# Attention and two feed-forward layers on one core: six raw weight tiles instead of five, one low-word buffer instead of two, three tiles of scaled first keys instead of four

## The chip, the core and the metric

The kernel runs on one core of one Trainium2 chip. The metric is the device time of one execution, in microseconds. TensorE (PE) does the matmuls and transposes, VectorE (DVE), ScalarE (ACT) and GpSimd (POOL) the elementwise work, and SyncE (SP) issues nearly all DMAs; PEld is the loading of weights into TensorE. Each engine works through its own list of instructions in order. An instruction that waits for a semaphore holds up everything behind it in its list.

## The reference

The inputs are q, k and v of 4 batches, 8 heads, 576 positions and 64 columns, a gate s per position, and five weight matrices in float32. What is computed, cut to what matters:

```python
cum  = cumsum(maximum(s, 0))
bias = minimum(-(cum[:, None] - cum[None, :]), 0)        # per head
a    = softmax(causal(q @ k.T / 8 + bias)) @ v           # 576 x 64 per head
x    = a, heads side by side                             # 2304 x 512
x    = (silu(x @ w_gate) * (x @ w_val)) @ w_out          # d_ff 1536
out  = silu(x @ w_in) @ w_out2                           # d_ff 2048
```

## The kernel before, in words

**Precision.** Every product is taken in three matmuls of the type fp32r: each operand is cut into a high part (rounded) and a low part (the rest), and high x high, high x low and low x high are summed in PSUM (`mm3`, L522 to L524). The rounding is a copy on ACT (L112), the rest a subtraction on POOL (L501 for weights, L535 for hidden units).

**Raw weight words.** The weights come from the host as 64-bit words, of which the device keeps 32 bits. A piece of 512 columns is loaded as a tile `r64` of 128 x 512 x 2 words (512 KB) and decoded: ACT writes the scaled high word into half of a 1024-column tile `zz` (L409) and the shifted low word into a buffer `dk` (L410); DVE joins the two (L412, L415). `r64`, `zz` and, later, the working tiles of the second layer's weights (`z32`, `s32`, `cut`) all live in one ring, the pool `raw`, 4 KB per partition each. One chunk of weights takes four `r64` and two `zz`. The buffer `dk` is in the pool `dec` for chunk 0 and for the second layer's weights (24 of 32 pieces); for the other chunks of the first layer it is a PSUM bank of the pool `ps_m`. That pool has four banks, and the outputs of the first layer's matmuls (`pgv`, `po`) and of the attention's value product (`pv`) take turns in the same four.

**Stages.** From 0 to about 60 us the attention of batch 0 runs alone. Then the first feed-forward layer runs batch by batch, nine chunks of weights each, with the attention of the next batch between its matmuls: a chunk takes about 18 us. During the nine chunks of batch 0 the next chunk is decoded and cut (`w_split`), the one after it loaded (`w_load`), and the cut weights are stored to DRAM (`w1_d`, L489) for batches 1 to 3. From about 233 us to 634 us the second layer's weights are decoded, combined, cut and stored (`ahead_load`, `ahead`, `u_sum`, `u_cut`, `u_store`). From about 640 us the second layer runs out of other tiles, laid where the first layer's were.

**Attention.** Per pair of heads there are two halves, A and B. For each tile of 128 queries: scores on PE (`psc`, L218), minimum with the gate on DVE (L235, result `m`), exponential on ACT (L255), the sum's inverse `rl` (L268), scaling of `e` on POOL (`normal`, L116), and, from batch 1 on, the first 64 keys scaled into an own tile `z` of 128 x 128 (`first_keys`, ACT for half A, POOL for half B). PE then transposes `e` and `z` into `ptr` (L302, L316), and multiplies by v (`pv`, L351). The small tiles `m`, `l`, `rl` are in the pool `sm`.

**What sets the order.** Up to about 60 us the order on every engine is that of the code. From there to the end of batch 2 PE's order is that of the code, and a scheduler places the instructions of ACT, DVE, POOL and SP by its own model of time and by when tiles of the pools come free (`manual_schedule(engines={PE})`). From the last batch of the first layer on, the order is again that of the code.

```python
# gate(), 2 banks per step, then silu_mul(): tanh on ACT (L531), (tanh + 1) * gate on DVE (L532), * value (L533)
for t in range(2):
    ps = ps_m.tile([P, 512], F32, tag="m", name="pgv")
# w_split(c): decode the four pieces, cut and store the two halves
# w_ahead(c), at the start of chunk c: w_split(c + 1), then w_load(c + 2)
```

Of the kernel before, what the change touches and what calls it, by code (L numbers as in the profile page):

```python
# [66 lines left out]
def kernel(  # L67
# [11 lines left out]
    first_layer = ctx.enter_context(ExitStack())  # L79
    attention = ctx.enter_context(ExitStack())  # L80
    second_layer = ctx.enter_context(ExitStack())

    def pool(name, bufs, space=None, scope=ctx, side="left"):
        kw = {"space": space} if space is not None else {}
        return scope.enter_context(tc.tile_pool(name=name, bufs=bufs, side=side, reuse_waits="tile", **kw))
# [2 lines left out]
    const = pool("const", 1)  # L88
    dram = pool("dram", 1, bass.MemoryType.DRAM)
    wt_p = pool("wt", 4)  # L90
    raw_p = pool("raw", 5, scope=first_layer)
    dec_p = pool("dec", 2, scope=first_layer)
    tmp_p = pool("tmp", 3, scope=first_layer)
    h_p = pool("h", 6, scope=first_layer)
    xt_p = pool("xt", 8, scope=first_layer)
# [1 line left out]
    qkr_p = pool("qkr", 3, scope=attention, side="right")  # L97
    cum_p = pool("cum", 3, scope=attention, side="right")
    e_p = pool("e", 6, scope=attention, side="right")
    z_p = pool("z", 4, scope=attention, side="right")  # L100
    pt_p = pool("pt", 3, scope=attention, side="right")
    zero_p = pool("zero", 1, scope=attention, side="right")
    v_p = pool("v", 2, scope=attention, side="right")
    sm_p = pool("sm", 10, scope=attention, side="right")
    ps_m = pool("ps_m", 4, PS)
    ps_a = pool("ps_a", 2, PS, scope=attention, side="right")

# [959 lines left out]
```

## Time and profile before

| what | us |
|---|---|
| three runs | 1009.87, 1007.95, 1001.23 |
| their median | 1007.95 |
| the profiled execution | 1002.95 |
| its span, first to last instruction | 1001.1 |
| PE busy / PEld busy | 989.5 / 929.8 |
| POOL, DVE, ACT busy | 592.7, 557.0, 523.0 |
| mean granted clock of TensorE | 0.998 |

The profiled execution is 5.0 us under the median of the three runs, which lie 8.6 us apart. A row of the trace gives an instruction's start in us from the span's start, its duration, its engine and source line, what it writes and reads, and in brackets how long its engine had been idle before it and which instruction ended that. Names are those of the program's tiles, without their numbers (`r` is an `r64`, `wraw` a `zz`, `w_d` is `w1_d`).

### The profile page before, as it was taken

How to read it: one execution, taken by the hardware profiler on the slowest of the kernel's cores; microseconds unless marked ns; L12 is line 12 of the kernel's file. 1: busy time of each engine (PE TensorE's matmuls, PEld its weight loads, DVE VectorE, ACT ScalarE, POOL GpSimd, SP SyncE). 2: the span in 40 equal slices, each digit the busy share in tenths (PEclk: the TensorE clock that was granted, in tenths of full speed). 3: DMA queues.
4: the chain of work that ended last, by engine and by line, in shares of the span. 5: the costliest groups of instructions: out<-in, count | busy, mean ns of one | idle time of the engine just before them, and what ended most of it. 6: DMA issues, size and time to landing. Idle time of an engine off the chain costs nothing.

```text
span 1001.1 us, 19462 instructions
## 1 busy us (share of the span) xinstructions
PE 989.5 (99%) x6924; PEld 929.8 (93%) x6924; DVE 557.0 (56%) x1408; ACT 523.0 (52%) x1267; POOL 592.7 (59%) x748
## 2 busy tenths in 40 slices
PE   8999999999999999999999999999999999999998
PEld 6588889999998899899899999999999999999998
DVE  6868576635546545535542323366666667665555
ACT  6779888535666436655533443234544335543333
POOL 6967747515867556757542665356567458674445
PEclk9999999999999999999999999999999999999999
DMA  8798879667779799775858776797767866896662
GB/s 240 198 319 301 275 277 301 222 221 246 279 267 294 266 306 311 265 248 214 288 205 330 270 297 258 261 388 278 294 242 281 312 222 249 297 343 232 244 219 113
DMA packets 81616, 267.16 MB, mean 267 GB/s; under 512 B 9904, under 2 KB 29360, under 8 KB 66160
## 3 DMA queue, kind: packets, MB, share of 16 engines
q1 hardware_dynamic: 81328, 265.66, 75.8%
q8 instruction: 54, 0.88, 0.3%
q14 instruction: 42, 0.34, 0.1%
q10 hardware_dynamic: 192, 0.27, 0.1%
HBM read 208.15 MB, written 57.75 MB: 266 GB/s over the span
## 4 chain that ended last, share of the span: by engine, by line
PE 90%; ACT 3%; DMA 3%; DVE 2%; issue 1%; POOL 1%; SPq 0%; DVEq 0%; ACTq 0%; POOLq 0%
PE pgv L522 9%; PE pgv L524 9%; PE pgv L523 9%; PE pu L663 6%; PE pu L666 6%; PE pu L667 6%; PE po L708 6%; PE po L709 6%; PE po L710 6%; PE po L522 5%; PE po L523 5%; PE po L524 5%; PE pv L351 5%; PE psc L218 4%; PE ptr L302 3%; ACT e L255 1%
## 5 line engine op out<-in xcount | busy, mean ns | idle before, releaser
L522 PE MATMUL pgv<-xt,wt 128*128 128x288 f32 x768 | 229.5, 299 | 0.2 <-DVE wraw L415 0.2
L524 PE MATMUL pgv<-xt,wt 128*128 128x288 f32 x768 | 226.1, 294 | 0.0
L523 PE MATMUL pgv<-xt,wt 128*128 128x288 f32 x768 | 226.0, 294 | 0.0
L640 POOL TENSOR_TENSOR h<-u,h 128x384 fp32r<-128x384 f32 x72 | 74.8, 1039 | 142.1 <-ACT h L112 134.5
L522 PEld LDWEIGHTS pgv<-xt,wt 128*128 128x128 f32 x768 | 144.1, 188 | 11.5 <-DVE m L235 6.3
L523 PEld LDWEIGHTS pgv<-xt,wt 128*128 128x128 f32 x768 | 144.1, 188 | 0.0
L524 PEld LDWEIGHTS pgv<-xt,wt 128*128 128x128 f32 x768 | 144.0, 188 | 0.0
L112 ACT ACTIVATE h<-u 128x288 fp32r<-128x288 f32 (+1 forms) x168 | 79.8, 475 | 100.5 <-DVE u L533 99.2
L535 POOL TENSOR_TENSOR h<-u,h 128x288 fp32r<-128x288 f32 x96 | 79.0, 825 | 86.4 <-ACT h L112 84.2
L522 PE MATMUL po<-h,wt 128*128 128x288 f32 x384 | 114.7, 299 | 0.0
L523 PE MATMUL po<-h,wt 128*128 128x288 f32 x384 | 113.1, 294 | 0.0
L524 PE MATMUL po<-h,wt 128*128 128x288 f32 x384 | 113.0, 294 | 0.0
L708 PE MATMUL po<-h,wt 128*128 128x384 f32 x336 | 112.4, 335 | 0.0
L709 PE MATMUL po<-h,wt 128*128 128x384 f32 x336 | 112.3, 334 | 0.0
L710 PE MATMUL po<-h,wt 128*128 128x384 f32 x336 | 112.3, 334 | 0.0
L663 PE MATMUL pu<-x,wt 128*128 128x384 f32 x330 | 111.8, 339 | 0.1
L666 PE MATMUL pu<-x,wt 128*128 128x384 f32 x330 | 111.8, 339 | 0.0
L667 PE MATMUL pu<-x,wt 128*128 128x384 f32 x330 | 111.7, 339 | 0.0
L640 POOL TENSOR_TENSOR h<-t,h 128x384 fp32r<-128x384 f32 x96 | 107.0, 1136 | 5.5 <-ACT h L112 5.5
L669 ACT ACTIVATE s<-pu 128x384 f32<-128x384 f32 x48 | 23.6, 492 | 150.0 <-PE pu L667 150.0
L255 ACT ACTIVATE e<-e,m 64x64 f32<-64x64 f32 (+4 forms) x160 | 88.3, 554 | 25.7 <-DVE m L235 25.0
L719 DVE TENSOR_TENSOR acc<-po,acc 128x384 f32<-128x384 f32 x144 | 76.8, 558 | 36.3 <-PE po L710 35.6
(115 smaller groups left out, 2187.0 us busy)
## 6 DMA issues: line engine op xcount, KB each, us to landing
wt<-w_d SPq DMA_DIRECT2D x54, 1024.0 KB, 6.9
wt<-wu_d SPq DMA_DIRECT2D x48, 1024.0 KB, 9.2
wt<-wu_d SPq DMA_DIRECT2D x47, 768.0 KB, 6.8
r<-in_w_dram SPq DMA_DIRECT2D x36, 512.0 KB, 6.8
w_d<-wt SPq DMA_DIRECT2D x18, 1024.0 KB, 8.5
r<-in_w_dram SPq DMA_DIRECT2D x64, 256.0 KB, 7.1
qkr<-in_qk_dram SPq DMA_DIRECT2D x32, 288.0 KB, 9.0
cumb<-cum_d SPq DMA_DIRECT2D x15, 576.0 KB, 9.2
```

Of the source, the lines that this page charges most:

```text
L112: act_last[:] = [nc.scalar.activation(out=out, in_=in_, func=AF.Copy, scale=scale).ins]
L255: nc.scalar.activation(out=e[:r, hd, :wd], in_=e[:r, hd, :wd], func=AF.Exp, bias=m[hd][:r], scale=-1.0, accum_out=put[hd],)
L522: nc.tensor.matmul(out=ps[:, :n], lhsT=a, rhs=xh, start=(k == 0), stop=False)
L523: nc.tensor.matmul(out=ps[:, :n], lhsT=a, rhs=xl, start=False, stop=False)
L524: nc.tensor.matmul(out=ps[:, :n], lhsT=c, rhs=xh, start=False, stop=(k == last))
L640: nc.gpsimd.tensor_tensor(out=h[:, 1], in0=u, in1=h[:, 0].bitcast(F32), op=ALU.subtract)
L663: nc.tensor.matmul(out=o, lhsT=a, rhs=x[:, 0, kk], start=fresh and kk == 0, stop=False, skip_group_check=True)
L666: nc.tensor.matmul(out=o, lhsT=a, rhs=x[:, 1, kk], stop=False, **more)
L667: nc.tensor.matmul(out=o, lhsT=c, rhs=x[:, 0, kk], stop=kk == 1, **more)
L708: nc.tensor.matmul(out=ps, lhsT=a, rhs=h[:, 0], start=fresh, stop=False, skip_group_check=True)
L709: nc.tensor.matmul(out=ps, lhsT=a, rhs=h[:, 1], stop=False, **more)
L710: nc.tensor.matmul(out=ps, lhsT=c, rhs=h[:, 0], stop=e == 1, **more)
```

## The change

Four numbers of tiles in pools: `raw` 5 to 6, `dec` 2 to 1, `z` 4 to 3, `sm` 10 to 8.

```diff
-    raw_p = pool("raw", 5, scope=first_layer)
-    dec_p = pool("dec", 2, scope=first_layer)
+    raw_p = pool("raw", 6, scope=first_layer)
+    dec_p = pool("dec", 1, scope=first_layer)
...
-    z_p = pool("z", 4, scope=attention, side="right")
+    z_p = pool("z", 3, scope=attention, side="right")
...
-    sm_p = pool("sm", 10, scope=attention, side="right")
+    sm_p = pool("sm", 8, scope=attention, side="right")
```

PE's list of 5749 rows is the same in both kernels. On ACT, DVE, POOL and SP the lists are the same up to about 60 us, and from there to the end of batch 2 the scheduler places instructions differently, mostly in the nine chunks of batch 0. In the rows below a tile's number tells it apart: `r64_1101`, `1103`, `1105`, `1107` are the four pieces of chunk 2, `r64_1295` to `1301` those of chunk 3; `u_1259` is the result of the last gate step of chunk 0, `u_1474` that of the third of chunk 1.

The list of ACT at the start of chunk 1 (about 70 to 78 us), before:

```order
L531 ACTIVATE u_1168<-pgv_1142 128x288
L409 ACTIVATE wraw_1265<-r64_1101 128x512
L409 ACTIVATE wraw_1265<-r64_1103 128x512
L112 ACTIVATE h_1030<-u_1168 128x288
L410 ACTIVATE dk_1266<-r64_1101 128x512
L410 ACTIVATE dk_1271<-r64_1103 128x512
...
L255 ACTIVATE e_1011,l_1222<-e_1011,m_1218 128x320
L531 ACTIVATE u_1259<-pgv_1233 128x288
L255 ACTIVATE e_1011,l_1222<-e_1011,m_1220 128x320
```

and with the change:

```order
L409 ACTIVATE wraw_1265<-r64_1101 128x512
L409 ACTIVATE wraw_1265<-r64_1103 128x512
L112 ACTIVATE h_1109<-u_1136 128x288
L531 ACTIVATE u_1168<-pgv_1142 128x288
L409 ACTIVATE wraw_1276<-r64_1105 128x512
L409 ACTIVATE wraw_1276<-r64_1107 128x512
L112 ACTIVATE h_1030<-u_1168 128x288
...
L255 ACTIVATE e_1011,l_1222<-e_1011,m_1218 128x320
L255 ACTIVATE e_1011,l_1222<-e_1011,m_1220 128x320
L531 ACTIVATE u_1259<-pgv_1233 128x288
```

All four high words are now taken ahead of `h_1030`, where two were, and the tanh of `u_1259` stands behind both exponentials of 128x320 instead of between them.

The list of ACT in the second half of chunk 1 (about 86 to 95 us), before:

```order
L112 ACTIVATE pt_1443<-ptr_1432 128x2x384
L267 ACTIVATE l_1356<-l_1356 128x2
L112 ACTIVATE h_1367<-u_1426 128x288
L409 ACTIVATE wraw_1512<-r64_1295 128x512
L409 ACTIVATE wraw_1512<-r64_1297 128x512
L531 ACTIVATE u_1474<-pgv_1448 128x288
L410 ACTIVATE dk_1513<-r64_1295 128x512
...
L409 ACTIVATE wraw_1523<-r64_1299 128x512
```

and with the change:

```order
L409 ACTIVATE wraw_1523<-r64_1299 128x512
L409 ACTIVATE wraw_1523<-r64_1301 128x512
L267 ACTIVATE l_1356<-l_1356 128x2
L112 ACTIVATE pt_1443<-ptr_1432 128x2x384
L112 ACTIVATE h_1367<-u_1426 128x288
L531 ACTIVATE u_1474<-pgv_1448 128x288
L410 ACTIVATE dk_1513<-r64_1295 128x512
```

The last two pieces of chunk 3 are read ahead of the tanh of `u_1474`, where they stood behind it.

The list of POOL in chunk 1 (about 78 to 91 us), as the difference:

```order
 L116 TENSOR_SCALAR e_1004<-e_1004,rl_1210 128x128 x2
+L116 TENSOR_SCALAR e_1011<-e_1011,rl_1225 128x256 x2
 L501 TENSOR_TENSOR wt_1287<-wraw_1265,wt_1287 128x1024
 L200 AFFINE_SELECT e_1566<-cumb_784 128x192 x2
 L535 TENSOR_TENSOR h_1109<-u_1259,h_1109 128x288
-L116 TENSOR_SCALAR e_1011<-e_1011,rl_1225 128x256 x2
 L501 TENSOR_TENSOR wt_1291<-wraw_1276,wt_1291 128x1024
```

The scaling of the last `e` tile of the half goes ahead of a weight cut, two masks and an `h`. In the same way SP issues the loads of chunk 3's last two pieces (`r64_1299`, `r64_1301`) ahead of the store of a cut weight tile that stood between them, and POOL writes the second `z` of a half B behind the masks of the next half instead of ahead of them.

## Rows read from the trace of the kernel before

**Rows 1.** Busy us (instructions) by stretch: PE, PEld, DVE, ACT, POOL, PEclk, DMA share, GB/s.

```profile
16.00:58.00 42.00, 39.06 (x337) 25.27 (x338) 34.22 (x131) 33.07 (x88) 39.06 (x72) 0.96 0.85 251
58.00:110.00 52.00, 51.06 (x394) 46.20 (x394) 37.27 (x106) 45.06 (x115) 34.42 (x51) 1.00 0.88 301
110.00:390.00 280.00, 280.00 (x2175) 254.33 (x2174) 154.22 (x471) 164.88 (x430) 160.25 (x242) 1.00 0.80 269
...
640.00:990.00 350.00, 349.90 (x2006) 349.61 (x2005) 218.03 (x370) 150.24 (x326) 204.97 (x182) 1.00 0.74 272
```

**Rows 2.** What PE waited for: us in total, times, longest us.

```profile
PE ptr L302 <- POOL e L116: 3.5, 6, 1.4
...
PE pgv L522 <- DVE wraw L415: 0.2, 1, 0.2
```

**Rows 3.** PE in order of time, four starts of groups of matmuls.

```profile
77.99 0.40 PE L522 MATMUL pgv<-xt,wt 128*128 128x288 f32 x1
...
85.46 1.00 PE L302 MATMUL ptr<-ident,e 128*128 128x128 f32 x4 [0.63 <-POOL e L116]
...
94.62 0.40 PE L522 MATMUL pgv<-xt,wt 128*128 128x288 f32 x1 [0.19 <-DVE wraw L415]
...
412.22 0.76 PE L351 MATMUL pv<-pt,vz 128*64 128x320 f32 x4 [0.61 <-DVE u L532]
```

**Rows 4.** DVE in order of time: what frees the banks of Rows 3.

```profile
77.51 0.43 DVE L532 SCALAR_TENSOR_TENSOR u<-u,pgv 128x288 f32<-128x288 f32 x1
...
93.88 0.68 DVE L415 SCALAR_TENSOR_TENSOR wraw<-r,dk 128x512 uint32<-128x512 uint32 x1
```

**Rows 5.** ACT in order of time, chunk 1.

```profile
72.66 0.67 ACT L409 ACTIVATE wraw<-r 128x512 f32<-128x512 f32 x1 [0.98 <-DMA r<-in_w_dram]
73.23 0.43 ACT L112 ACTIVATE h<-u 128x288 fp32r<-128x288 f32 x1
...
76.86 0.38 ACT L531 ACTIVATE u<-pgv 128x288 f32<-128x288 f32 x1
77.15 0.55 ACT L255 ACTIVATE e<-e,m 128x320 f32<-128x320 f32 x1
...
88.72 1.24 ACT L409 ACTIVATE wraw<-r 128x512 f32<-128x512 f32 x2
89.85 0.41 ACT L531 ACTIVATE u<-pgv 128x288 f32<-128x288 f32 x1
```

**Rows 6.** Issue of raw loads; us to landing, issued at 63.3, 66.5, 84.0.

```profile
66.09 1.39 SPq L388 DMA_DIRECT2D r<-in_w_dram  x2
...
r<-in_w_dram SPq DMA_DIRECT2D x1, 512.0 KB, 4.7
...
r<-in_w_dram SPq DMA_DIRECT2D x2, 512.0 KB, 6.7
...
r<-in_w_dram SPq DMA_DIRECT2D x1, 512.0 KB, 10.8
```

**Rows 7.** Stretches as in Rows 1: ACT in chunk 1; TensorE's clock.

```profile
78.00:90.00 12.00, 11.25 (x85) 10.82 (x84) 8.78 (x34) 12.00 (x32) 9.57 (x14) 1.00 0.85 256
...
14.00:16.00 2.00, 0.41 (x2) 0.14 (x1) 1.95 (x11) 1.72 (x6) 2.00 (x5) 1.00 0.85 227
...
18.00:20.00 2.00, 2.00 (x10) 0.98 (x10) 1.97 (x12) 2.00 (x7) 2.00 (x5) 0.50 1.04 289
```

**Rows 8.** What ACT waited for after 240 us, as in Rows 2.

```profile
ACT cut L112 <- DMA wu_d<-cut: 19.0, 7, 4.7
```

**Rows 9.** Buffer dk: DVE's last use of one, ACT's next write.

```profile
17.43 1.01 DVE L415 SCALAR_TENSOR_TENSOR wraw<-r,dk 128x512 uint32<-128x512 uint32 x1
...
18.76 0.65 ACT L410 ACTIVATE dk<-r 128x512 uint32<-128x512 uint32 x1
```

**Rows 10.** A half B's second z; the transposes that free its tile.

```profile
120.91 0.60 POOL L116 TENSOR_SCALAR z<-e,rl 128x64 f32<-128x64 f32 x2 [0.50 <-DVE rl L268]
...
122.19 0.49 PE L316 MATMUL ptr<-ident,z 128*128 128x128 f32 x3
```

## The prediction

> **What bounds the kernel now.** I read the table of stretches first. From 110 to 390 us and from 640 to 990 PE is busy all the time, at a granted clock of 1.00; gaps of more than a microsecond lie ahead of 110 [rows 1] or at the very end, where nothing is changed. The reader is to see that there is almost nothing to win on the other engines: ACT, DVE and POOL are busy half of the time, and each of their delays costs something only where it reaches PE. So I read next what PE waited for [rows 2]. The largest entry, 3.5 us in six waits for a scaled `e`, lies almost wholly before 60 us, where the order of every engine is that of the code. Behind 60 us just three waits are left, and the order in time shows them: 0.63 us at 85.46, 0.19 at 94.62 and 0.61 at 412.22 [rows 3]. Together that is 1.43 us, 0.14% of the time, and it is all that a better order behind 60 us can give back. PE's own list is unchanged, so no matmul is added or removed. A change in time must be a wait of PE that goes or comes.
>
> **The change part by part.** I measure against the profiled execution, 1002.95 us.
>
> *Sixth raw tile, in the first layer.* It frees the loads from the ring's tail and lets the scheduler take all four high words of a chunk earlier on ACT. What this meets is thin: the four PSUM banks that decoding shares with the matmuls. At 77.99 us PE starts chunk 1's first gate in the bank that the tanh of `u_1259` and DVE's multiply behind it have just left: DVE's L532 runs from 77.51 for 0.43, so the bank is free at 77.94 [rows 4], 0.05 us ahead of PE [rows 3]. There is no slack here, and the view of waits doesn't say so because nothing was late. Now I move ACT's list. Before, ACT waited 0.98 us for the second piece, read it at 72.66 and came to `h` at 73.23: a read is worth 0.57 [rows 5]. With the change ACT must have the third and fourth piece too before that `h`. They are issued no earlier than about 66.1 (the engine order puts two small loads ahead of them as before), and such a load landed after 4.7, 6.7 or 10.8 us [rows 6]. At 6.7, the middle one and that of the two loads issued at this very place, ACT has the third at 72.8 and is through both at 72.8 + 2 x 0.57 = 73.9, 0.7 late. The tanh then also stands behind one more exponential of 0.55 [rows 5]. 0.7 + 0.55 = 1.25 us: tanh at 78.1 instead of 76.86, bank free at 79.2, PE's gate at 79.2. **+1.25.** Bounds: at 4.7 us ACT is early by more than the exponential costs, so 0; at 10.8 us it is 4.1 us later, so 5.3.
>
> *The scaling of `e` moved ahead on POOL.* The 0.63 us at 85.46 is PE waiting for just the instruction that now stands ahead of the weight cut. **-0.63**, at worst 0. The weight cut that was ahead of it comes later by this one pair of instructions; PE first reads those weights when it starts chunk 2, at 94.62 [rows 3], and that lies nine microseconds behind. If this cover were gone, the chunk's start would be late by the length of the pair, which I bound by the 1.00 us that PE spent on the four transposes it releases.
>
> *Two more reads ahead of the tanh of `u_1474`.* ACT is full from 78 to 90 us, 12.00 of 12 [rows 7]. So it cannot make up the 1.25, and the pair of reads now ahead of the tanh adds what the pair at 88.72 took, 89.85 - 88.72 = 1.13 [rows 5]. Tanh at 89.85 + 2.4. The chain from it ends in DVE's L415 at 93.88, which frees the bank of PE's start at 94.62 [rows 3, 4]; PE was already 0.19 late there. All 2.4 pass through: PE starts chunk 2 at 97.0 instead of 94.62. Of these 2.4 us, 1.25 - 0.63 = 0.62 are already counted, so **+1.78** here. Bounds: 0, if DVE takes up the lateness, since the low words of the last two pieces are no longer interleaved with reads; and about 6, if the last piece again takes the 10.8 us it took behind a store [rows 6]. That store is now issued after it, hence the lower middle.
>
> *Later chunks of batch 0.* The same moves, but PE waited for a decode nowhere else: the entry is one wait of 0.2 us [rows 2]. Nothing in the sum; the price if this cover is gone is the third rival.
>
> *Sixth raw tile, in the second layer's weights.* ACT waited 19.0 us in seven waits for stores to leave tiles of the ring [rows 8]. Only one delay of this kind reached PE, at 412.22. With six tiles for the six that one round needs, it should go. **-0.61**, at worst 0.
>
> *One `dk`.* At the start DVE's last use of the other buffer ends at 18.44, and ACT writes the next at 18.76 [rows 9]: 0.3 us of cover; lost cover would cost one such DVE instruction, 1.0 us. In the second layer's weights pieces are a quarter of a chunk apart. 0.
>
> *Three `z`.* The second `z` of half B was written at 120.91, and the transposes that free its new tile are at 122.19 [rows 10]. It would wait 1.8 us on POOL with `e` behind it; the scheduler has put it behind the masks, so the wait falls where POOL has nothing PE needs soon. The reader is PE a chunk, 18 us, later. 0; the price if it blocked is that 1.8 us once. *Eight small tiles:* a minimum now waits for the exponential eight minima back instead of ten; 0.
>
> **Sum:** 1.25 - 0.63 + 1.78 - 0.61 = +1.8, so 1004.7 against the profiled 1002.95. That execution lies 5.0 us under the median of the runs, 1007.95, and the runs spread over 8.6 us without a cause in this profile. I take the middle of both for what three runs will show: 1004.7 + 2.5 = **1007**. This spread also says that about 1% is what can be told from no change.
>
> TensorE's clock fell to 0.50 from 18 to 20 us, the lower of its two levels, 1.2 instead of 2.4 GHz, after PE had been busy for only 0.41 of the 2 us from 14 to 16 [rows 7]; that cost half of 2 us. From 58 to 110 us, with the 0.63 us wait in it, it stayed at 1.00 [rows 1]. So I add nothing for the clock. The Trainium skill, "TensorE: Matmul & The Clock Gate", section "HAM oscillation — how this bites in real kernels", says that a PE that waits between groups of matmuls is slowed and starts the next group cold. By that rule my two new waits would each cost about the 1.0 us of that drop more, 1006.7 on the profiled base.
>
> **Rivals.** *Nothing reaches PE* (0.27): the loads land early, DVE absorbs the rest, or the sixth tile is not what the loads wait for at all, so that the change does not do what it says. Then only the three waits move: between -1.43 and 0, 1001.5 to 1003 on the profiled base, 1004 to 1005.5 in runs. For it: margins in the scheduler's plan are not mine; against it: the 0.05 us.
>
> *PE is not really full* (0.03). Loading of weights is busy 46.2 of 52 us and 254.3 of 280 us [rows 1], 31 us short in both; if a third of it were waits that the ring causes, the time would fall by 10 us, to 992. Against it: PE does 2175 matmuls in 280 us and 2006 in 350, where loading is full; the first are the narrower ones and go at 129 ns each, and 394 in the 51.1 busy us of 58 to 110 at 130, the same pace on both sides of the gaps. The Trainium skill, "Perfetto Trace Analysis", section "Identifying the Most-Contended Engine", says that matmul busy time is no good measure of the distance from the limit and names weight loading instead. By that rule these 31 us are headroom; the pace says it isn't waiting.
>
> *Slower* (0.08): the same late tanh at each start of chunks 3 to 8 as at chunk 2. The place is the shared banks; the price is 1.78 each, six times, 10.7 us: 1015.4 on the profiled base, 1018 in runs. It decides from the point at which ACT is as full as in chunk 1. Against it: 58 to 110 us holds 45 us of ACT in 52, later 165 in 280 [rows 1].
>
> **How the numbers follow.** My forecast has 0.62. The range starts at the lowest run less the three waits, 1001.23 - 1.43 = 999.8, and ends at the highest run plus half of the upper bounds' 6 us, about 1013; the slower rival and the headroom stay outside. Faster by over 1% needs the second rival or a lucky set of runs: 0.04. Slower by over 1% is the third rival and a little for the upper bounds: 0.09. The rest, 0.87, is within 1%.
>
> **What would show it.** In the changed profile PE should wait about 1.2 us for DVE at the first gate of chunk 1, near 78 us, and about 2 us at the start of chunk 2, near 95 to 97; the waits at 85 and 412 should be gone; ACT's waits for stores after 240 us should fall well under 19 us; PE should be busy all the time from 110 us on. It is wrong if PE waits in every chunk, if the end at 990 to 1001 us is longer, or if the waits before 60 us change, where no instruction moved.

## The result and the profile after

The changed kernel takes 1013.33 us, the median of 8 runs (1012.01 to 1014.77), against 1004.33 us of the kernel before in the same comparison (8 runs, 1001.23 to 1009.87): a ratio of 1.0087, 95% interval 1.0072 to 1.0101. It is slower by 9.0 us, where 1.8 us was forecast. The forecast time itself, 1007.0, stood on a higher base, since the three runs known then had a median of 1007.95; even so the result lies 0.3 us above the end of its range.

The profiled execution has a span of 1011.6 us. First the table of stretches, with the columns of [rows 1]:

```profile
16.00:58.00 42.00, 37.33 (x315) 23.96 (x314) 36.59 (x130) 31.57 (x86) 35.92 (x64) 0.92 0.79 242
58.00:110.00 52.00, 48.61 (x378) 43.34 (x379) 34.27 (x102) 43.47 (x109) 34.59 (x54) 1.00 0.88 295
110.00:390.00 280.00, 275.94 (x2133) 250.49 (x2133) 149.58 (x461) 162.87 (x423) 157.11 (x241) 0.99 0.78 260
640.00:990.00 350.00, 349.94 (x2025) 349.65 (x2024) 214.54 (x365) 147.15 (x318) 203.12 (x179) 1.00 0.75 277
```

From 640 us on nothing is different. From 58 to 390 us PE was idle for 0.9 us before and is idle for 7.5 us now; the clock has fallen somewhere behind 110 us; and from 16 to 58 us, where no instruction moved, PE was busy for 1.7 us less, at a mean clock of 0.92 instead of 0.96. The four largest of PE's waits behind 58 us (columns of [rows 2]; four shorter ones come to 1.8 us):

```profile
PE po L522 <- DVE xt L366: 2.0, 1, 2.0
PE pgv L522 <- DVE wraw L415: 1.5, 1, 1.5
PE pgv L522 <- DVE u L532: 1.5, 1, 1.5
PE po L522 <- DVE wraw L415: 1.2, 1, 1.2
```

Two of these four are the ones forecast, at the starts of chunks 1 and 2; two were not. In order of time, those two starts, which answer to the first and third row of [rows 3]:

```profile
82.68 0.41 PE L522 MATMUL pgv<-xt,wt 128*128 128x288 f32 x1 [1.49 <-DVE u L532]
...
99.46 0.41 PE L522 MATMUL pgv<-xt,wt 128*128 128x288 f32 x1 [1.52 <-DVE wraw L415]
```

The matmul at 82.68 reads `xt` and `wt`. It has no use for `u`, which DVE's L532 writes; what links them is the PSUM bank that L532 reads. The same holds for L415 and `dk`. On ACT, ahead of the tanh at 81.68 (compare [rows 5]):

```profile
74.87 0.68 ACT L409 ACTIVATE wraw<-r 128x512 f32<-128x512 f32 x1 [2.05 <-DMA r<-in_w_dram]
76.95 0.67 ACT L409 ACTIVATE wraw<-r 128x512 f32<-128x512 f32 x1 [1.40 <-DMA r<-in_w_dram]
77.51 0.44 ACT L112 ACTIVATE h<-u 128x288 fp32r<-128x288 f32 x1
```

These are the two reads that moved ahead of `h`. (All times here are 2.6 us late against the profile of before, which PE lost before 58 us.) Each stands at the head of ACT's list before its load has landed, and holds up everything behind it. The view of ACT's waits from 58 to 190 us adds this up; first before, then after:

```profile
ACT wraw L409 <- DMA r<-in_w_dram: 1.5, 2, 1.0
```

```profile
ACT wraw L409 <- DMA r<-in_w_dram: 16.2, 10, 4.3
```

This row is the one to see. The loads did not become slower (28 of them landed 6.7 us after issue at the median before, 5.4 after); the reads now come earlier than the landings. The longest of the ten waits reaches PE at the end of chunk 3; the next, 3.33 us at 170.29, does so in chunk 6, through L415, 1.24 us at 176.86. ACT, DVE and PE at the first place:

```profile
133.07 0.66 ACT L409 ACTIVATE wraw<-r 128x512 f32<-128x512 f32 x1 [4.29 <-DMA r<-in_w_dram]
133.63 0.37 ACT L112 ACTIVATE xt<-pv 128x256 fp32r<-128x256 f32 x1
```

```profile
134.04 0.42 DVE L366 TENSOR_TENSOR xt<-pv,xt 128x256 fp32r<-128x256 f32 x1 [5.36 <-ACT xt L112]
```

```profile
134.52 0.40 PE L522 MATMUL po<-h,wt 128*128 128x288 f32 x1 [1.96 <-DVE xt L366]
```

A read waits 4.29 us; the copy of the attention's result that stands behind it is late; DVE's subtraction behind that is late; it frees the bank that PE wants for `po`. In the kernel before, the same instruction of DVE was done long ahead:

```profile
122.04 0.42 DVE L366 TENSOR_TENSOR xt<-pv,xt 128x256 fp32r<-128x256 f32 x1 [1.22 <-ACT xt L112]
```

The bank was free at 122.46 and PE came to it at 127.26: even 4.8 us of cover were used up. In the changed kernel, right behind the wait at 134.52, TensorE's clock falls to its lower level, 1.2 instead of 2.4 GHz, for 3.4 us (two stretches, the columns as above):

```profile
128.00:136.00 8.00, 6.04 (x46) 5.82 (x45) 1.29 (x4) 3.67 (x10) 3.26 (x8) 1.00 1.02 278
136.00:139.40 3.40, 3.40 (x17) 2.26 (x16) 3.27 (x6) 2.79 (x5) 0.00 (x0) 0.50 0.78 251
```

PE's list is the same in all kernels here (6924 matmuls in each profile), so a matmul can be followed from profile to profile. This table is worked out so: how much later than in the first profile of the kernel before the same matmul starts, in us. The heads are its times in that profile.

```
                       42.4   75.2   78.6   86.2   95.1  127.1  132.2  165.5  170.9  395.2  421.6  700.0
after                 +2.65  +2.62  +4.70  +3.52  +4.86  +5.14  +8.92  +9.73 +11.03 +11.03 +10.35 +10.16
after, again          +1.79  +1.77  +3.46  +2.27  +3.32  +3.38  +5.70  +7.34 +10.57 +10.58  +9.89 +10.82
start_dk              -0.08  -0.08  +1.81  +0.62  +2.17  +2.30  +5.11  +6.57  +9.80  +9.80  +9.12 +10.51
pin                   +1.87  +1.87  +1.82  +0.63  +0.47  +1.09  +1.09  +1.09  +1.09  +1.09  +0.41  +0.92
no_raw6               +0.60  +0.57  +0.52  -0.53  -0.50  -0.04  -0.04  -0.04  -0.04  -0.04  -0.19  +0.25
pin23                 +1.26  +1.29  +1.24  +0.06  -0.14  +0.51  +2.37  +4.47  +6.20  +6.20  +5.51  +6.09
pin_upper             -0.01  -0.02  -0.07  -1.26  -0.23  -0.21  -0.21  -0.21  -0.21  -0.21  -0.90  +0.14
words_in_sbuf         +1.86  +1.85  +2.43  +2.99  +3.23  +9.36  +9.42 +14.66 +14.66 +14.66 +13.97 +13.89
pin_start_dk          +1.38  +1.36  +1.31  +0.12  -0.05  -0.03  -0.03  -0.03  -0.03  -0.03  -0.72  +0.09
act_work              +2.91  +2.91  +3.68  +2.49  +7.59  +8.89  +8.90  +8.93  +8.87  +8.97  +8.70  +8.70
own_sixth             -0.03  -0.02  -0.06  -0.71  -0.70  -0.69  -0.70  -0.70  -0.69  -0.69  -1.38  +0.01
before, again         +0.88  +0.89  +0.86  +0.83  +0.86  +0.86  +0.86  +0.86  +0.86  +0.86  +1.20  +3.42
```

Read along the first row: chunk 1's start costs 2.1, POOL's moved scaling gives 1.2 back, chunk 2's start costs 1.3, chunks 3 to 6 cost 6.2, and the second layer's weights give 0.7 back. Two stretches vary from execution to execution whatever the kernel: the one before 42 us, and that from 422 to 700, where the two profiles of the kernel before differ by 2.2 us (1.58 of it is one wait of PE at 597.51 for weights read back from DRAM; eight of the thirteen profiles have that wait, 0.34 to 1.58 us long). What a change does is read between them.

### The profile page after: what moved, and what is told of

It reads as the page before. It is cut to its first block, busy times and chain, and to the rows that moved or that the text cites. A ratio compares the mean times of both kernels' runs of the same rounds, so it can differ in the third digit from the quotient of the medians.

```text
span 1011.6 us, 19469 instructions
## 1 busy us (share of the span) xinstructions
PE 992.1 (98%) x6924; PEld 931.5 (92%) x6924; DVE 561.3 (55%) x1408; ACT 524.2 (52%) x1267; POOL 592.6 (59%) x748
## 4 chain that ended last, share of the span: by engine, by line
PE 85%; DMA 6%; DVE 4%; ACT 3%; issue 1%; POOL 0%; SPq 0%; DVEq 0%; ACTq 0%
PE pgv L522 8%; PE pgv L524 8%; PE pgv L523 8%; PE pu L663 6%; PE pu L667 6%; PE pu L666 6%; PE po L708 6%; PE po L709 6%; PE po L710 6%; PE po L522 5%; PE po L523 5%; PE po L524 5%; PE pv L351 4%; DMA r<-in_w_dram 4%; PE psc L218 3%; PE ptr L302 3%
## 5 line engine op out<-in xcount | busy, mean ns | idle before, releaser
L116 POOL TENSOR_SCALAR e<-e,rl 128x128 f32<-128x128 f32 (+8 forms) x135 | 72.8, 555 | 47.9 <-DVE rl L268 45.4
```

## The experiments

Eleven more runs were made, two of them of the changed kernel and the kernel before once more, in three sets, each beside the kernel before (medians 1004.46, 1003.76 and 1004.7 us). Theory A: ACT's early reads delay what stands behind them, and PE waits at the shared banks. Its rivals are named with each.

| kernel | us, median | against before, 95% interval |
|---|---|---|
| pin | 1003.2 | 0.9991 [0.9981, 1.0001] |
| no_raw6 | 1004.05 | 1.0002 [0.9987, 1.0016] |
| start_dk | 1013.65 | 1.0090 [1.0077, 1.0103] |
| after, again | 1014.72 | 1.0102 [1.0089, 1.0115] |
| pin23 | 1009.91 | 1.0055 [1.0034, 1.0075] |
| pin_upper | 1003.68 | 0.9997 [0.9983, 1.0011] |
| words_in_sbuf | 1016.37 | 1.0120 [1.0097, 1.0144] |
| pin_start_dk | 1002.83 | 0.9984 [0.9969, 0.9999] |
| act_work | 1013.44 | 1.0089 [1.0074, 1.0104] |
| own_sixth | 1003.41 | 0.9986 [0.9974, 0.9999] |
| before, again | 1006.38 (one run) | |

**pin.** The changed kernel with ACT's list put back. `tanhs` collects the tanh instructions as they are written; the block orders issue on ACT alone and waits for nothing.

```
-        unpack(zz, t, k, part)
+        with tc.issue_after(tanhs[-1 if e > 1 else -2 if c == 2 else -3]) if 1 < c < len(L1) else nullcontext():
+            unpack(zz, t, k, part)
```

> The changed kernel, all four pool sizes as changed, but ACT's list in batch 0 put back: a chunk's reads of high words stand behind the same tanh as in the kernel before. Theory A (ACT's early reads delay the tanh whose bank PE wants): the steps of PE's lateness at the starts of chunks 1, 2 and at the ends of chunks 3 and 5 (1.6, 1.3, 2.1 and 1.3 us) go, and the 3.4 us stretch of half clock behind chunk 3 with them; left are the start-up's +2.65 and the second layer's -0.7, so about 2 us over the kernel before, 1005 to 1008. Rival B (the sixth tile's loads and their DMA traffic, or the shorter z and sm rings, make PE wait whatever ACT's list is): 1011 to 1014, with PE's waits for DVE still in chunks 1 to 6.

Measured: 1003.2, no different from the kernel before. Its stretches and its row of ACT's waits:

```profile
58.00:110.00 52.00, 51.97 (x407) 47.10 (x404) 37.21 (x107) 45.01 (x115) 36.34 (x58) 1.00 0.90 307
110.00:390.00 280.00, 279.65 (x2175) 254.51 (x2176) 151.60 (x468) 165.61 (x429) 157.71 (x241) 1.00 0.80 268
```

```profile
ACT wraw L409 <- DMA r<-in_w_dram: 4.0, 3, 2.7
```

The pool sizes are the same, and from 60 to 190 us ACT makes 32 reads of high words as in the changed kernel; yet PE is full again but for 0.4 us, at a full clock. The loss hangs on the place of the reads in ACT's list, and rival B falls. (The edit holds ACT's list alone; the scheduler places the other engines' instructions by it anew, and what of the gain passes through them was not held apart.) The start-up is 1.87 us late in this profile too, but the median shows none of it: the 2 us that were left for it in the expectation were too much.

**no_raw6.** The change without the sixth tile.

```
-    raw_p = pool("raw", 6, scope=first_layer)
+    raw_p = pool("raw", 5, scope=first_layer)
```

> The change without its sixth raw tile: five raw tiles, one low-word buffer, three z, eight small tiles. Theory A: only the start-up's part of the loss is left, at most 2.65 us, and the wait at 412 us is back: 1004 to 1007. Rival B in its second half (z and sm rings): 1011 to 1014. If the start-up's part is chance and not the single low-word buffer: 1003.5 to 1005.

Measured: 1004.05, level. One low-word buffer, three `z` and eight small tiles together cost nothing that can be measured.

**start_dk and after, again.** Chunk 0's low words in other tiles; and the changed kernel a second time.

```
         else:
-            k = dec_p.tile([P, DW], U32, tag="dk", name="dk")
+            k = h_p.tile([P, 2, S], U32, tag="h", name="dk")[:, 0, :DW]
```

> The changed kernel with one thing more: the four low-word buffers of chunk 0 are tiles of the ring of h, which is free until 59 us, so that at the start no low word waits for the one before; from 190 us on the single buffer serves as in the change. No engine's list differs from the changed kernel. Theory S (the single buffer costs the start-up 2.65 us): no wait of ACT for DVE near 19.6 us, PE's lateness against the kernel before under 0.5 us at 45 us, and about 2.5 us less than the changed kernel: 1010 to 1011.5. If the start-up's lateness comes from DVE's slow instructions beside POOL or from the clock's phase alone: as the changed kernel, 1012.5 to 1014.

> The changed kernel once more, for a second profile of it. All theories: 1012 to 1015, and about 9 us over the kernel before. Theory A: the four steps of lateness behind 58 us stand again, within 0.5 us each. Open is whether the start-up's 2.65 us and the half-clock stretch behind chunk 3 stand in a second execution; if they are chance, lateness at 45 us lies anywhere from 0 to 2.65 us.

Measured: 1013.65 and 1014.72; the intervals overlap. Theory S wanted 2.5 us less than the changed kernel, and start_dk takes 0.3 us more than the changed kernel's first set of runs and 1.1 less than its second: S falls. Of the changed kernel's steps, those at chunks 1 and 2 stand again within 0.5 us; the wait at the end of chunk 3 is 1.0 us instead of 2.0, and the half clock comes at chunk 6, so that the expectation missed there. In the first profile of the changed kernel ACT did wait for the one buffer; in the second it did not, and the start-up was 1.79 us late all the same. The two profiles' rows of the second low word:

```profile
19.60 0.68 ACT L410 ACTIVATE dk<-r 128x512 uint32<-128x512 uint32 x1 [1.24 <-DVE wraw L415]
```

```profile
17.45 0.66 ACT L410 ACTIVATE dk<-r 128x512 uint32<-128x512 uint32 x1
```

Over the thirteen profiles the lateness at 42 us lies between -0.03 and 2.91 us in the nine with one buffer at the start, and between -0.08 and 1.38 us in the four without. It varies with the execution, and most of it goes with a single long L415 of DVE in chunk 0. In the four profiles where the third L415 takes 2.93 us instead of 0.8 (after, again, pin, act_work) the lateness steps up by 1.8 us between 36 and 42 us; in the two where the second takes 2.7 (words_in_sbuf, pin_start_dk) by 1.6 us between 24 and 30. With 1.25 and 1.45 us for the third (pin23, no_raw6) the step is 0.6 us; no other profile has one there. pin_start_dk has no single buffer at the start. A part for the single buffer, in how often this happens, stays open. Of the table, the three profiles with the changed list of ACT agree from 75 us on: 8.4, 8.8 and 9.9 us lost by 171 us.

**pin23 and pin_upper.** Two doses of the first experiment: the list put back only for the two chunks of weights that are decoded first, `c in (2, 3)`; and only for a chunk's last two pieces, `e > 1`, in all chunks.

> The changed kernel with ACT's reads of high words put back behind the old tanh for the third and fourth chunk of weights only (those decoded during chunks 1 and 2); the later chunks keep the early reads. Theory A, each early read costing on its own: the steps at the starts of chunks 1 and 2 (1.5 to 1.65 and 1.0 to 1.5 us in three profiles) go, those from the end of chunk 3 on stay with the half-clock stretch, 5.5 to 7 us; 3 us less than the changed kernel, about 1010.5. Theory D (PE's lateness gives the loads and decodes a head start, so what is lost early is saved later): with PE 2 to 3 us earlier, the later steps grow by about 1 us, 1011.5 to 1013. If the loss were one thing that needs all chunks: 1003 to 1005.

> The changed kernel with only the reads of a chunk's third and fourth piece held behind the last tanh ahead of them, in all chunks of batch 0; the first two pieces are read as early as the scheduler likes. Theory A says that these two are what the sixth tile let move, so that most of the loss goes: 1004 to 1007. If the first two pieces, which moved ahead of one more tanh in chunks 2, 3 and 6, cost as much: 1007.5 to 1010.

Measured: pin23 6.15 us over the kernel before. The steps at 78 and 95 us are gone. Those from 127 to 171 us come to 5.7 us, without a stretch of half clock; with the whole change they come to 5.9, 7.2 and 7.5 us, or 4.4, 5.8 and 6.1 less the 1.4 to 1.5 us of that stretch. What is lost early is not repaid later: the time is under theory D's 1011.5 to 1013, and D falls, though against the first profile alone the later steps are 1.3 us longer. Its waits of PE:

```profile
PE po L522 <- DVE wraw L415: 1.6, 1, 1.6
PE pgv L522 <- DVE wraw L415: 1.0, 1, 1.0
PE pgv L522 <- DVE xt L366: 1.0, 1, 1.0
```

pin_upper is level with the kernel before, just under what was expected. ACT still waits for loads in five reads, 3.7 us in all and 1.5 at the longest, and PE once, 1.2 us at the start of chunk 2, which the moved scaling ahead of it pays for. So it is the last two pieces, whose loads are issued last, that cost the time.

**words_in_sbuf.** Low words of chunks 1 to 8 out of PSUM.

```
-        if 0 < c < len(L1):
+        if False:
```

> The changed kernel with the low words of chunks 1 to 8 in the one low-word buffer instead of in the four PSUM banks that the matmuls use too; ACT's list still has two or more reads ahead of the old tanh in most chunks, and each low word now waits for the one before to be used. Theory A with the shared bank as the way to PE: with four banks for the gates alone, a tanh may be 5 us late before PE waits; no wait of PE for the decode's last step (L415), the waits for L532 go or shrink under 0.5 us: 1003 to 1007. If it is ACT's or DVE's lateness itself that reaches PE, whatever bank it holds: waits of 1 us and more at the chunk starts stay, 1009 to 1015; the single buffer could add its own through late weights (PE waiting for wt).

Measured: 1016.37, a miss, with 10.2 us at half clock behind 100 us in its profile. PE waits for L415 nowhere any more, as the shared bank would have it, but the one buffer makes a new wait on ACT, of 10.5 us, which delays the tanh in its turn. ACT's row, and PE's:

```profile
ACT dk L410 <- DVE wraw L415: 10.5, 12, 1.6
```

```profile
PE pv L351 <- DVE u L532: 3.5, 2, 2.7
PE pgv L522 <- DVE u L532: 2.0, 2, 1.8
PE pgv L522 <- DVE u L533: 1.3, 1, 1.3
```

It doesn't test the banks by themselves: two things changed at once. That they are the link rests on which tiles the waiting matmuls read.

**act_work.** Does the time of the reads matter, or the wait for their loads? The kernel of no_raw6 with work added on ACT that waits for no load.

```
+            more = b == 0 and len(hs) > 1 and nc.scalar.activation(
+                out=more_p.tile([P, 3, HB], F32, tag="more", name="more")[:, :, :n], func=AF.Copy,
+                in_=pg[:, :n].rearrange("p (o n) -> p o n", o=1).to_broadcast([P, 3, n]),
+            )
+            with tc.issue_after(more.ins) if more else nullcontext():
                 nc.scalar.activation(out=u, in_=pg[:, :n], func=AF.Tanh, scale=0.5)
```

> The kernel with five raw tiles, one low-word buffer, three z and eight small tiles, its reads where they were, and one piece of work more for ACT: right ahead of each tanh of batch 0 (from the first chunk's second step on) it copies the same PSUM bank three times over into a tile that nobody reads, 128x864, by the rows of 512 and 288 columns about 1 us, close to the 1.13 us of a pair of reads. No load is waited for. Theory W (it is ACT's waiting for loads that have not landed, 16.2 us against 1.5, that delays the tanh): small steps of lateness, under 0.5 us each, 1004 to 1008. Theory T (the time of the two reads themselves is enough): steps of about 1 us at most chunk starts, as in the changed kernel, 1010 to 1015; 28 tanh at 1 us each would be far more if every one of them reached PE.

Measured: 1013.44, but in a form that neither theory had expected. The added copies (23 instructions, not the 28 of the expectation; min/median/max in ns), the stretches, ACT's waits for loads, and the one long wait of PE:

```profile
L531 ACT ACTIVATE more<-pgv x23: 866/892/944, 69.5 to 207.6; 128x864 f32<-128x864 f32 x23
```

```profile
58.00:110.00 52.00, 46.05 (x343) 41.57 (x343) 32.97 (x100) 47.52 (x114) 32.64 (x52) 0.93 0.83 276
110.00:390.00 280.00, 280.00 (x2183) 254.91 (x2182) 154.45 (x467) 176.66 (x446) 163.19 (x246) 1.00 0.78 267
```

```profile
ACT wraw L409 <- DMA r<-in_w_dram: 1.7, 3, 0.9
```

```profile
PE pgv L522 <- DVE wraw L415: 4.9, 1, 4.9
```

Up to chunk 2's start ACT has no time to spare, the copies pile up, and PE waits 4.9 us once, with a stretch of half clock that begins in it and lasts 6.8 us. Behind 110 us the copies go on and PE loses nothing: 280.00 of 280.00. So work on ACT alone costs in chunks 1 and 2 (theory T), and in chunks 3 to 6, where the changed kernel loses most, it is the waiting for landings (theory W). One reservation: PE here is already 8.9 us late, which may lend ACT some room. pin23 speaks against much of that: there PE is early again, and its later waits are no longer for it than in two of the three profiles of the whole change.

**pin_start_dk and own_sixth.** Two versions meant to beat both: the list put back and the start's low words elsewhere; and, without any pinning, a ring of five with the sixth tile as a buffer of its own for the second layer's sums.

```
-    raw_p = pool("raw", 6, scope=first_layer)
+    raw_p = pool("raw", 5, scope=first_layer)
+    six_p = pool("six", 1, scope=first_layer)
...
-        r = wst["d", q, "S"] = raw_p.tile([P, CW // 2], F32, tag="wraw", name="s32")
+        r = wst["d", q, "S"] = six_p.tile([P, CW // 2], F32, tag="six", name="s32")
```

> A version to beat both: six raw tiles, ACT's list of batch 0 put back, and chunk 0's low words in tiles of the ring of h. Against the kernel with the list put back alone (1003.2) it takes away the wait of ACT for DVE near 19.6 us; against the kernel before it keeps the gain at 412 us and at 85 us. Expected: lateness at 45 us against the profile of before under 0.5 us, PE full from 58 us on; 0.7 to 2 us less than the kernel before, 1002 to 1004. If the start-up's part is chance: as the list put back alone, 1003 to 1004.

> Five raw tiles, and the sixth as a buffer of its own for the sums of the second layer's weights alone, with one low-word buffer, three z and eight small tiles. The chunks of batch 0 then have the ring that they had. Theory A: no early read, PE's waits of chunks 1 to 6 gone without any order held by hand, and the wait at 412 us gone too: 1003 to 1005, level with the kernel before. If the sixth tile as such or the other rings cost: 1008 and more.

Measured: 1002.83 and 1003.41, both under the kernel before by about 0.15%, the intervals ending just under 1. pin_start_dk's start-up was 1.38 us late all the same, where under 0.5 was expected. own_sixth from 58 us on:

```profile
58.00:110.00 52.00, 51.69 (x399) 46.80 (x397) 37.37 (x106) 44.96 (x115) 34.44 (x51) 1.00 0.89 306
110.00:390.00 280.00, 280.00 (x2175) 254.43 (x2174) 153.19 (x475) 166.23 (x431) 159.48 (x243) 1.00 0.80 271
```

The gain of the sixth tile is small: the 0.7 us at 412 us, which stands in the trace of every kernel that has the tile, and it can be had without the loss. In the times it is at the edge of what can be told: pin and pin_upper have it too, and 1 lies within their intervals; own_sixth's profile is 1.38 us ahead at 422 us and level at 700, by a wait for weights from DRAM that the second profile of the kernel before has as well.

**before, again.**

> The kernel before once more, for a second profile. If the start-up's lateness of 0 to 2.65 us at 45 us, seen in the runs so far whatever buffers they had, is chance, this profile may be late there too against the first one; behind 58 us PE's three short waits (0.63, 0.19, 0.61) should stand again and the clock should stay full: 1001 to 1008.

Measured: 1006.38, start-up 0.88 us late against the first profile, and no more than 0.06 us of change from 75 to 395 us; behind 421 us it loses 2.2 us more. The three waits stand again, 0.6, 0.2 and 1.0 us. What the changed kernel loses from 75 to 395 us stands far out of what these two executions differ by there.

## Why the prediction was right or wrong, point by point

- **PE is full, and a change is a wait that comes or goes.** Right; every difference could be read as such, but for the clock.
- **Chunk 1's start, +1.25.** Right in place, link and order of events; 2.1, 1.7 and 1.9 us in three profiles. The sum had both loads landing together at 72.8; the second is issued more than 1 us behind the first, and ACT waits for each. start_dk, whose start-up is level with the kernel before, shows it: through both at 74.64, not 73.9.

```profile
72.28 0.67 ACT L409 ACTIVATE wraw<-r 128x512 f32<-128x512 f32 x1 [2.08 <-DMA r<-in_w_dram]
74.07 0.66 ACT L409 ACTIVATE wraw<-r 128x512 f32<-128x512 f32 x1 [1.12 <-DMA r<-in_w_dram]
74.64 0.43 ACT L112 ACTIVATE h<-u 128x288 fp32r<-128x288 f32 x1
```

- **POOL's scaling, -0.63.** The wait went; 1.2 us came back, since the four transposes behind it, spread over 1.00 us before, now follow each other too.
- **Chunk 2's start, +1.78.** 1.3, 1.1 and 1.5 us. Right: through chunk 2 the sum had 2.4 us, and the three profiles lose 2.24, 1.55 and 2.25.
- **Later chunks of batch 0: "Nothing in the sum".** This is the step that failed: 6.2, 7.3 and 7.6 us from 95 to 171 us, the half clock among them. The sign that was named for it failed with it: PE is busy for 275.94 of 280 us from 110 us on, not all the time. The third rival had the shared banks and these chunks, at 10.7 us and a chance of 0.08, and was set aside because ACT is busy for only 165 of 280 us there. act_work shows that argument to be right for work, and the changed profile shows what it left out: an engine that takes its list in order can be held for 4.3 us by a load while it is not busy at all. That PE had waited for a decode nowhere else before said nothing on it either, since only two reads came ahead of their landing then, 1.5 us in all. The landing times were read for the starts of chunks 1 and 2 alone [rows 6].
- **Second layer's weights, -0.61.** Right: -0.7 in every kernel with the tile, and ACT's wait for stores fell from 19.0 us [rows 8] to one entry of 2.6 us in the changed kernel.
- **One `dk`, 0.** The cover of 0.3 us was lost in one profile, with a wait of 1.24 us, and not in another. In the times it can't be told.
- **Three `z`, eight small tiles, 0.** Right as far as the time of no_raw6 tells, which holds them together with the one `dk`.
- **The clock, 0.** Wrong in size. All three profiles with the changed list have one stretch of 3.4 us at 0.50 behind 58 us, once behind chunk 3's wait and twice behind chunk 6's; by the steps of lateness inside it, each took 1.4 to 1.5 us. It is not in every execution: the mean granted clock, on record for each run, is 0.998 in four of the changed kernel's eight (1012.0 to 1013.8 us), which leaves room for 3 to 5 us at half clock in all, and the start alone takes 3.4 or 6.8 in every profile. So the waits alone carry most of the loss. The price of a fall was misread too: the one in [rows 7] does not cost half of 2 us, since the clock is 0.90 from 16 to 18 us and 0.74 from 20 to 22 as well, 1.7 us in all. The Trainium skill, "TensorE: Matmul & The Clock Gate", section "HAM oscillation — how this bites in real kernels", describes a kernel whose PE waits for a DMA between groups of matmuls and starts each next group cold; those waits are longer than any that PE has behind 58 us in the changed kernel's profiles, so the prediction read more into it than it says when it applied it to waits of 1 to 2 us. The trace agrees in part: the waits of 1.2 to 1.7 us at chunks 1 and 2 brought no fall in any of the three. But the same wait of 1.65 us for `po` in chunk 6 stands ahead of a fall in "after, again" and start_dk, and ahead of none in pin23; what decides is not shown.
- **Before 60 us.** The text said that a change there would show it wrong. It is no sign of that: in the changed kernel's two profiles 1.8 us of the 2.65 and 1.79 lost there go with a single long L415, which a kernel without the single buffer shows as well, and the kernel before varies there by 0.9 us. A part for the single buffer stays open.
- **The base.** 1007 took the middle of the profile and the first three runs, 1005.5, as the time of before; eight runs have 1004.33.

In sum, of the 9.0 us the waits at chunks 1 and 2, 2.7 to 3.4 us, less 1.9 given back were forecast; the waits behind 95 us and the half clock with them, 6.2 to 7.6 us, were not; the rest varies with the execution, in the start-up and behind 422 us.

## What to carry to other kernels

When a larger ring lets a scheduler move an instruction that needs a load ahead in the list of an in-order engine, look up for each new place whether the load has landed by then; how busy the engine is does not answer that. Behind each such instruction, follow what it holds up to the PSUM bank that the matmuls take next. And where only one part of the program wants the extra buffer, give it to that part alone: the other part's order then stays as it was.

## What the runs showed of the hardware

DVE's L415, 0.68 us for 128x512 in most places, took between 0.69 and 3.24 us in its first three executions in the thirteen profiles, where POOL is at work nearly without a break. In the changed kernel's first profile the third ends at 39.58, and POOL's six instructions beside it, back to back, at 39.03 (DVE, then POOL):

```profile
36.65 2.93 DVE L415 SCALAR_TENSOR_TENSOR wraw<-r,dk 128x512 uint32<-128x512 uint32 x1
```

```profile
35.87 1.93 POOL L116 TENSOR_SCALAR e<-e,rl 64x64 f32<-64x64 f32 x4
37.75 1.28 POOL L200 TENSOR_SCALAR_AFFINE_SELECT e<-cumb 128x576 f32<-128x576 f32 x2
```

All that took 0.79 us or more end like this, 0.5 to 0.75 us after one of POOL's instructions has ended; the five of 0.69 began with POOL idle or just beginning. That reads as DVE held until POOL lets it in, but no run varies it by itself, and why it is let in behind the first of POOL's instructions in one profile and behind the sixth in another is not shown. The first L415, which frees the buffer of [rows 9], took 1.01 us before and this in the changed kernel, which is why a cover of 0.3 us is none:

```profile
16.93 2.63 DVE L415 SCALAR_TENSOR_TENSOR wraw<-r,dk 128x512 uint32<-128x512 uint32 x1
```

The longest of the changed kernel's 28 raw loads between 58 and 190 us landed 11.6 us after issue and the shortest 3.7, of the same 512 KB.
